# One transition of a fused convolution and expert kernel: the last gate operations wait until block 0 is split

## The chip, the cores and the metric

The kernel runs on one NeuronCore of a Trainium2 chip. The metric is the device time of one execution in microseconds (us); three executions of the kernel before are given, and one more was taken with the hardware profiler. The engines are named as in the profile: PE is TensorE (its weight loads are PEld), DVE is VectorE, ACT is ScalarE, POOL is GpSimd, and SP is SyncE, which issues most of the DMA transfers.

## The reference

A long causal convolution by FFT feeds a two-level mixture of experts. Cut to what matters:

```python
Xf = np.fft.rfft(x, n=2 * S, axis=1)                  # x: (8, 5056, 128)
Hf = np.fft.rfft(h, n=2 * S, axis=0)                  # h: (5056, 128)
x = np.fft.irfft(Xf * Hf[None], n=2 * S, axis=1)[:, :S].reshape(B * S, D)
g_logits = x @ w_group;  g_idx = argmax(g_logits, 1)  # 4 groups, softmax weight g_w
for g in range(4):
    xg = x[g_idx == g]
    e_logits = xg @ w_expert[g]; e_idx = argmax(e_logits, 1)  # 4 experts, weight e_w
    for e in range(4):                                # rows of that expert
        h = np.maximum(xe @ w1[g, e], 0.0)            # 128 -> 1024
        out[tok_idx] = (g_w * e_w)[:, None] * (h @ w2[g, e])  # 1024 -> 128
```

## The kernel before

The eight sequences and the filter h go through in three rounds of three. A round has a first stage (`stage1`, a transform of length 158, 96 steps), then `groups`: for each of 40 pairs of frequencies a forward transform on PE (line 522), two products y and m with the filter's spectrum on DVE (line 540), their sum (line 574), an inverse transform on PE (line 589) and a copy zs on ACT (line 599), which goes to DRAM. The pairs go two by two through a slot of eleven list entries with weights `GW`, 2.0 at the entries 6 and 10 and else 0; so there are 20 slots, p = 0, 2, ..., 38, and a 21st of inverse transforms and stores alone, whose eleven entries (`late(2)`) are run among the first steps of the expert blocks.

A round's second half is its `side`: eight column groups, each with two lumps of inverse transform on PE (lines 723 and 737), transposes and copies of rows (lines 780, 781), the gate's logits (790, 800), and then `gate_math`: some 38 small operations, mostly on DVE (lines 898 to 989), that find each row's expert and its place, with four small count matmuls (lines 975, 976) after eight empty steps. When they are done, the rows are stored by `scatter`, one indirect transfer of POOL for each of 15 columns, with a small cast `pos` before it (line 855, on ACT or DVE); `send` issues the next of them, and `drain` all that are left. A gate operation counts as small: if the list has entries of weight 0 ahead, it is kept in `light` and run one or a few at a time after such entries.

The order of all this is written out: `run` builds one list `main` of (weight, function), and `weave` runs it and lets each side's steps fall due as the weight of the list goes by, from the side's start to its end. The side of round r goes beside round r + 1. The middle side (round two's) starts in round three's first stage and ends at `mark["end", 1]`, which is step 16 - `SIDE1` of the expert blocks.

After round three, `turn` closes the buffers of the rounds and opens those of the experts, `ffn_first(0)` transposes block 0's rows x and splits x and two pieces of its weights in two parts each (a cast on ACT, a subtraction on DVE; lines 1301, 1302), and then the blocks of 512 rows follow with eight steps each: step k does three matmuls of the first layer (`mm1`, lines 1357 to 1359), the split of its result h (lines 1362, 1363), and three of the second layer for two steps before (`mm2`, 1375 to 1377). In steps 0 to 7 of block 0 other splits of weights and of block 1's x fall as well. A block needs a table that tells its expert and its rows; block 0 to 3 have theirs from round one's counts. `table_a`, for the blocks from 4 on, is run seven entries to a step (`NTA`) from the step after the middle side's end: a count `nblocks` with empty entries before its matmul (line 1017), then some 25 small DVE operations, a store of the table to DRAM and a load back (lines 1088, 1093), both on SP. At step 16 SP loads block 4's x (line 1257), which waits for all stores of rounds one and two; `drain` stands at step 15. From step 14 on the last side's lumps run beside the blocks.

Of the kernel before, what the change touches and what calls it, by code (L numbers as in the profile page):

```python
# [46 lines left out]
GW = [0, 0, 0, 0, 0, 0, 2.0, 0, 0, 0, 2.0]  # L47
FW = [0, 0, 1.0, 0, 0, 0, 1.0, 0]
W_S1, W_END = 0.45, 2.5
SIDE0, SIDE1, SIDE2 = 10, 14, 24  # L50
SLOTS = 56
LATE = 4
END0 = 20
# [25 lines left out]
NQ = (NG + 1) // 2  # L79
# [96 lines left out]
def weave(main, sides):  # L176


    light = []

    def flush(n):
        for f in light[:n]:
            f()
        del light[:n]

    room = [0] * (len(main) + 1)
    for i in reversed(range(len(main))):
        room[i] = room[i + 1] + 1 if main[i][0] == 0 else 0
    for i, (w, f) in enumerate(main):
        f()  # L190
        if w == 0:
            flush(-(-len(light) // room[i]))
        for s in sides:
            if s["start"] <= i < s["end"]:
                if i == s["start"]:
                    s["done"] = 0
                    s["acc"] = s["sacc"] = 0.0
                    s["len"] = sum(w for w, _ in main[s["start"]:s["end"]])
                    s["total"] = sum(x[0] for x in s["steps"])
                s["acc"] += w / s["len"]  # L200
                while s["done"] < len(s["steps"]) and (s["sacc"] < s["acc"] * s["total"] - 1e-6 or i == s["end"] - 1):
                    sw, sf, small = s["steps"][s["done"]]
                    if small and room[i + 1] > 0 and i < s["end"] - 1:
                        light.append(sf)
                    else:
                        if small:
                            flush(len(light))
                        sf()
                    s["sacc"] += sw
                    s["done"] += 1  # L210
                if i == s["end"] - 1:
                    flush(len(light))
# [18 lines left out]
class Kernel:  # L231
# [777 lines left out]
    def nblocks(self, x, name):  # L1009
        nc, cp = self.nc, self.tp()  # L1010
        t = cp.tile([128, NE], BF16, name=name + "_m")
        nc.vector.tensor_scalar(t, x, self.iop512, None, op0=ALU.is_gt)
        yield
        for _ in range(8):
            yield
        pr = self.routed()
        nc.tensor.matmul(pr[:, 0:NE], lhsT=self.ones, rhs=t, start=True, stop=True)
        nb = cp.tile([128, NE], F32, name=name)
        nc.vector.tensor_copy(out=nb, in_=pr[:, 0:NE])
        yield  # L1020
        return nb
# [604 lines left out]
    def run(self):  # L1626
        tc = self.tc
        with ExitStack() as ctx:
            self.pools(ctx)
            with ExitStack() as c2:  # L1630
# [7 lines left out]
                side = [self.side(r) for r in range(3)]  # L1638
                main, mark = [], {}

                def add(f, w=0.0):
                    main.append((w, f))

                def late(r):
                    return [f for p in gr[r][1][NQ // 2:] for _, f in p]

                def advance(g):
                    return lambda: next(g, None)
# [11 lines left out]
                for r in range(3):  # L1660
                    if r == 1:
                        add(self.share)
                    pre, steps = gr[r]
                    rest = late(r - 1) if r > 0 else []
                    n = len(s1[r][1])
                    t0 = self.table_0()
                    for k, f in enumerate(s1[r][1]):
                        add(f, W_S1)
                        if r > 0 and k % 2 == 1:
                            add(self.send)  # L1670
                        if r == 0:
                            add(advance(more))
                        if r == 2 and ("end", 0) in mark:
                            add(advance(t0))
                        if k >= 1:
                            for g in rest[RP * k - RP:RP * k]:
                                add(g)
                        if k == SIDE0 and r > 0:
                            add(side[r - 1][0])
                        if k == max(SIDE0 + SIDEG, END0 if r == 2 else 0) and r > 0:  # L1680
                            mark["start", r - 1] = len(main)
                            if r == 2:
                                mark["end", 0] = len(main)
                        if k >= n - PRE and (k - n) % 5 == 0:
                            add(advance(pre))
                    if r > 0:
                        add(lambda: None, W_END)
                    for p in range(0, NQ, 2):
                        for w, f in steps[p // 2]:
                            add(f, w)  # L1690
                        if p >= NQ - LOAD1:
                            add(advance(s1[r + 1][0] if r < 2 else early))
                add(turn)
                add(lambda: self.ffn_first(0))
                rest = late(2)
                ta, tq, tb, fill = self.table_a(), self.table_c(), self.table_b(), self.fill_rows()
                ahead = self.ffn_ahead()
                steps = [f for j in range(NW_MIN) for f in self.ffn_steps(j, (BLK, None) if j else None, NW_MAX)]
                for k, f in enumerate(steps):
# [34 lines left out]
                    if k % 8 == 0 and 0 <= m < TAKE and (m + 1) * n // TAKE > m * n // TAKE:  # L1734
                        add(lambda i=m * n // TAKE: self.take(i))
                weave(main, [
                    dict(start=mark["start", r], end=mark["end", r], steps=side[r][1]) for r in range(3)
                ])
                self.ffn_tail()

# [26 lines left out]
```

## Time and profile before

| | |
|---|---|
| three executions | 1806.07 us median (1799.17, 1806.07, 1806.64) |
| profiled execution | 1805.8 us, its span 1804.1 us |
| PE busy | 1697.4 us, 94% of the span |
| DVE busy | 1298.9 us, 72% |
| ACT busy | 1045.3 us, 58% |
| POOL busy | 759.9 us, 42% |
| mean granted PE clock | 0.979 |

The profiled execution is one of the program on the chip; the span is from its first to its last instruction, and the device time lies 1.7 us above it. Busy is the time in which an engine has at least one instruction at work; the ends of matmuls are modelled, so a busy PE is not a PE at its peak. The granted clock is the share of PE's full 2.4 GHz that the throttle let through.

### The profile page before, as it was taken

What the parts mean: (1) busy time and instruction counts of PE and PEld (TensorE: products, weight loads), DVE (VectorE), ACT (ScalarE), POOL (GpSimd) and SP (SyncE); (2) the same over time, 40 slices, a digit from 0 to 9 for tenths busy, and PEclk for the clock granted to TensorE, in tenths of its full rate; (3) what the DMA queues carried; (4) which work ended last, traced back from release to release, by engine and by line L of the source; (5) the groups of instructions that cost most, each with busy time, mean ns of one, the idle gap of its engine ahead of it and who ended that gap; (6) DMA issues with size and microseconds to landing.
All of it is one profiled execution on the core that took longest, in us unless ns stands there. A gap on an engine that the chain in (4) does not pass through costs nothing. (4 is left out here: it accounts for less than half of the span.)

```text
span 1804.1 us, 49057 instructions
## 1 busy us (share of the span) xinstructions
PE 1697.4 (94%) x17369; PEld 1315.7 (73%) x17369; DVE 1298.9 (72%) x2999; ACT 1045.3 (58%) x2554; POOL 759.9 (42%) x730
## 2 busy tenths in 40 slices
PE   8999888988899888999999999999999999999997
PEld 7667755556665554788777788787788877888987
DVE  6554577774567667677777778777788778787876
ACT  4554443443434344566666667676677767666665
POOL 0451232333144444415454445344555555333444
PEclk9999998998989999999999999999999999999999
DMA  7697676766657766665565554355655575444555
GB/s 211 210 276 210 166 219 202 229 229 191 178 169 234 212 198 224 188 178 171 170 176 169 168 156 144 114 170 182 206 166 155 154 228 181 139 130 144 155 163 157
DMA packets 277994, 330.23 MB, mean 183 GB/s; under 512 B 31863, under 2 KB 210304, under 8 KB 277720
## 3 DMA queue, kind: packets, MB, share of 16 engines
q1 hardware_dynamic: 248856, 270.93, 50.9%
q0 software_dynamic: 20608, 41.79, 6.7%
q10 hardware_dynamic: 8256, 14.10, 2.7%
q8 instruction: 143, 2.34, 0.6%
q14 instruction: 131, 1.07, 0.2%
HBM read 230.35 MB, written 96.86 MB: 181 GB/s over the span
## 5 line engine op out<-in xcount | busy, mean ns | idle before, releaser
L856 POOL DMA_INDIRECT srt<-rw,pos x320 | 339.7, 1062 | 503.8 <-ACT pos L855 130.9
L1428 POOL DMA_INDIRECT out<-orow,at x176 | 182.8, 1038 | 252.9 <-ACT at L1426 199.8
L540 DVE TENSOR_TENSOR y<-pp,hg 128x768 f32<-128x768 f32 (+1 forms) x120 | 103.7, 864 | 123.3 <-PE pp L522 48.0
L1428 POOL DMA_INDIRECT out<-orow,sids x92 | 95.7, 1041 | 123.8 <-DVE orow L1395 79.7
L589 PE MATMUL pp<-y,cg 64*128 64x384 f32 (+1 forms) x752 | 127.9, 466 | 12.9 <-DVE m L540 6.1
L522 PE MATMUL pp<-st,cg 64*64 64x192 f32 (+1 forms) x1588 | 122.4, 416 | 9.1 <-issue 9.0
L599 ACT COPY zs<-pp 128x768 f32<-128x768 f32 (+1 forms) x118 | 85.2, 723 | 72.6 <-PE pp L589 49.5
L439 DVE TENSOR_TENSOR st<-pp,odd 128x320 f32<-128x320 f32 x96 | 46.8, 488 | 101.5 <-ACT odd L438 97.4
L744 ACT COPY yT<-py 128x474 f32<-128x474 f32 (+1 forms) x96 | 44.5, 514 | 124.9 <-PE py L737 108.0
L723 PE MATMUL py<-ig,zm 126*64 126x79 f32 x2048 | 96.7, 241 | 17.2 <-issue 15.5
L1362 ACT ACTIVATE h0h<-px 128x512 fp32r<-128x512 f32 (+1 forms) x109 | 64.0, 587 | 84.3 <-PE px L1359 55.7
L1363 DVE SCALAR_TENSOR_TENSOR h0l<-px,h0h 128x512 fp32r<-128x512 f32 (+1 forms) x109 | 73.3, 673 | 54.5 <-ACT h0h L1362 35.2
L589 PEld LDWEIGHTS pp<-y,cg 64*128 64x128 f32 x752 | 71.9, 190 | 54.0 <-issue 27.6
L723 PEld LDWEIGHTS py<-ig,zm 126*64 126x64 f32 x2048 | 81.6, 141 | 39.4 <-issue 30.9
L540 DVE TENSOR_TENSOR m<-pp,hg 128x768 f32<-128x768 f32 (+1 forms) x120 | 102.7, 856 | 0.2 <-ACT hg L532 0.2
L522 PEld LDWEIGHTS pp<-st,cg 64*64 64x64 f32 x1588 | 60.9, 135 | 55.3 <-issue 42.4
L1363 DVE SCALAR_TENSOR_TENSOR h2l<-px,h2h 128x512 fp32r<-128x512 f32 (+1 forms) x112 | 75.3, 672 | 31.7 <-ACT h2h L1362 18.8
L1363 DVE SCALAR_TENSOR_TENSOR h3l<-px,h3h 128x512 fp32r<-128x512 f32 (+1 forms) x111 | 74.4, 671 | 27.5 <-ACT h3h L1362 26.3
L574 POOL TENSOR_TENSOR y<-y,m 128x512 f32<-128x512 f32 x40 | 50.8, 1275 | 83.0 <-DVE m L562 44.4
L1362 ACT ACTIVATE h3h<-px 128x512 fp32r<-128x512 f32 (+1 forms) x111 | 65.4, 589 | 33.6 <-PE px L1359 24.9
L1363 DVE SCALAR_TENSOR_TENSOR h1l<-px,h1h 128x512 fp32r<-128x512 f32 (+1 forms) x111 | 74.4, 671 | 9.0 <-ACT h1h L1362 3.0
L1362 ACT ACTIVATE h1h<-px 128x512 fp32r<-128x512 f32 (+1 forms) x111 | 65.3, 588 | 20.6 <-PE px L1359 11.5
(477 smaller groups left out, 5200.4 us busy)
## 6 DMA issues: line engine op xcount, KB each, us to landing
wr<-in_moe_w SPq DMA_DIRECT2D x373, 256.0 KB
zd<-zs SPq DMA_DIRECT2D x78, 384.0 KB
zm<-zd SPq DMA_DIRECT2D x64, 378.0 KB
cg<-in_c_g SPq DMA_DIRECT2D x106, 224.0 KB
xr<-srt SPq DMA_DIRECT2D x71, 260.0 KB
hg<-hd SPq DMA_DIRECT2D x80, 128.0 KB
zd<-zs SPq DMA_DIRECT2D x39, 256.0 KB
xt<-in_x ACTq DMA_DIRECT2D x52, 160.0 KB
```

Of the source, the lines that this page charges most:

```text
L439: nc.vector.tensor_tensor(out=all_st[:, 0:2 * HALF, d], in0=even, in1=odd, op=ALU.add)
L522: nc.tensor.matmul(px[c * 64:c * 64 + 64, b, to], lhsT=k, rhs=data[:, of], start=begin, stop=i == len(steps) - 1 or p == 0 and i == 1, til ...
L540: nc.vector.tensor_tensor(out=t[:, :, 0:w].rearrange("p t (r u d) -> p t r u d", r=2, u=nu), in0=taken(px, part).unsqueeze(1).broadcast_to ...
L574: (nc.gpsimd if r == 0 else nc.vector).tensor_tensor(out=y[:, :, 0:w], in0=y[:, :, 0:w], in1=m[:, :, 0:w], op=ALU.add)
L589: nc.tensor.matmul(pz[c][:, 0:w], lhsT=wt[c * 64:c * 64 + 64, k:k + 128], rhs=y[c * 64:c * 64 + 64, part, 0:w], start=part == 0, stop=part ...
L599: nc.scalar.copy(out=z[:, 0:n, 0:w], in_=pp[:, 0:n, 0:w])
L723: nc.tensor.matmul(pys[q][c:c + 64, col(n, u)], lhsT=zms[q][:, n % QB, k:k + 64], rhs=self.ig[:, 0:NH], start=n % QB == 0 and u == 0, stop ...
L744: nc.scalar.copy(out=self.yT[:, k:k + QB * c1], in_=pys.pop(q)[:, 0:QB * c1])
L856: ins = self.nc.gpsimd.indirect_dma_start(out=self.srt, out_offset=bass.IndirectOffsetOnAxis(ap=k["pos"][0:p, j:j + 1], axis=0), in_=k["rw ...
L1362: nc.scalar.activation(out=hh, in_=p, func=AF.Relu)
L1363: nc.vector.scalar_tensor_tensor(out=hl, in0=p, scalar=0.0, in1=hh.bitcast(F32), op0=ALU.max, op1=ALU.subtract)
L1428: ins = self.nc.gpsimd.indirect_dma_start(out=self.a["out"], out_offset=bass.IndirectOffsetOnAxis(ap=ids, axis=0), in_=o, in_offset=None, ...
```

## The change

Two things move. The middle side ends at step 5 of the expert blocks instead of step 2, and `table_a` starts three steps later with it. And from the entry of weight 2.0 at index 6 of round three's second last slot (p = 36) on, the middle side's small steps are kept in `light` without being run, until `ffn_first(0)` has been issued; from there to the side's end one of them is run after each entry of weight 0, and what is left then is run at the end of step 4. Large steps in the hold are run at once. In `table_a` (whose count is named nba) the count's matmul comes sixteen empty entries after its input instead of eight.

```diff
@@ -47,7 +47,7 @@
-SIDE0, SIDE1, SIDE2 = 10, 14, 24
+SIDE0, SIDE1, SIDE2 = 10, 11, 24
@@ -177,6 +177,7 @@
     light = []
+    holds = [s["hold"] for s in sides if "hold" in s]
@@ -188,8 +189,10 @@
     for i, (w, f) in enumerate(main):
         f()
-        if w == 0:
-            flush(-(-len(light) // room[i]))
+        held = any(a <= i < b for a, b in holds)
+        after = any(b <= i < s["end"] for s in sides if "hold" in s for b in (s["hold"][1],))
+        if w == 0 and not held:
+            flush(1 if after else -(-len(light) // room[i]))
@@ -200,10 +203,10 @@
                     sw, sf, small = s["steps"][s["done"]]
-                    if small and room[i + 1] > 0 and i < s["end"] - 1:
+                    if small and (room[i + 1] > 0 or held or after) and i < s["end"] - 1:
                         light.append(sf)
                     else:
-                        if small:
+                        if small and not held:
                             flush(len(light))
                         sf()
@@ -1011,7 +1014,7 @@
-        for _ in range(8):
+        for _ in range(16 if name == "nba" else 8):
             yield
@@ -1686,12 +1689,15 @@
                     for p in range(0, NQ, 2):
-                        for w, f in steps[p // 2]:
+                        for i, (w, f) in enumerate(steps[p // 2]):
+                            if r == 2 and p == NQ - 4 and i == 6:
+                                mark["hold"] = len(main)
                             add(f, w)
                 add(turn)
                 add(lambda: self.ffn_first(0))
+                mark["go"] = len(main)
@@ -1734,7 +1740,10 @@
                 weave(main, [
-                    dict(start=mark["start", r], end=mark["end", r], steps=side[r][1]) for r in range(3)
+                    dict(
+                        start=mark["start", r], end=mark["end", r], steps=side[r][1],
+                        **({"hold": (mark["hold"], mark["go"])} if r == 1 else {}),
+                    ) for r in range(3)
                 ])
```

## Rows read from the trace of the kernel before

**Rows 1.** the page, busy time, share of the span and instructions

```profile
PE 1697.4 (94%) x17369; PEld 1315.7 (73%) x17369; DVE 1298.9 (72%) x2999; ACT 1045.3 (58%) x2554; POOL 759.9 (42%) x730
```

**Rows 2.** timeline of PE: start, length, instruction, [idle before, its releaser]

```profile
708.16 1.20 PE L522 MATMUL pp<-st,cg 64*64 64x384 f32 x16 [1.95 <-issue]
709.16 0.67 PE L522 MATMUL pp<-st,ns 64*64 64x192 f32 x8
...
711.44 0.94 PE L522 MATMUL pp<-st,ns 64*64 64x192 f32 x8
712.31 1.80 PE L589 MATMUL pp<-y,cg 64*128 64x384 f32 x8
715.35 1.56 PE L589 MATMUL pp<-y,cg 64*128 64x384 f32 x8 [1.23 <-DVE m L540]
...
719.38 0.58 PE L1309 MATMUL ptr<-identr,xr 128*128 128x128 f32 x4 [2.14 <-DVE base L980]
```

**Rows 3.** timeline of DVE, last two slots to block 0's split

```profile
705.76 0.96 DVE L540 TENSOR_TENSOR y<-pp,hg 128x768 f32<-128x768 f32 x1 [2.76 <-PE pp L589]
706.64 0.56 DVE L928 TENSOR_REDUCE el<-oh 128x60 f32<-128x240 f32 x1
...
709.84 0.21 DVE L900 TENSOR_TENSOR td<-el,tmx 128x60 f32<-128x60 f32 x1
...
713.31 0.96 DVE L540 TENSOR_TENSOR y<-pp,hg 128x768 f32<-128x768 f32 x1
...
715.12 0.95 DVE L540 TENSOR_TENSOR y<-pp,hg 128x768 f32<-128x768 f32 x1
...
716.85 1.81 DVE L574 TENSOR_TENSOR y<-y,m 128x768 f32<-128x768 f32 x2
718.86 0.17 DVE L979 TENSOR_TENSOR off<-pp,base 128x16 f32<-128x16 f32 x1 [0.19 <-remote]
...
720.86 0.68 DVE L1302 TENSOR_TENSOR x0l<-ptr,x0h 128x512 fp32r<-128x512 f32 x1
```

**Rows 4.** timeline of ACT at the turn

```profile
718.15 0.80 ACT L599 COPY zs<-pp 128x768 f32<-128x768 f32 x1 [1.38 <-issue]
720.04 0.59 ACT L1301 CAST x0h<-ptr 128x512 fp32r<-128x512 f32 x1 [1.09 <-DVE cs L984]
```

**Rows 5.** windows: us, busy PE, PEld, DVE, ACT, POOL (instructions), clock, DMA, GB/s

```profile
720.86:738.81 17.95, 16.92 (x70) 11.37 (x66) 13.59 (x47) 11.88 (x28) 7.44 (x7) 0.94 0.84 238
738.81:748.31 9.50, 9.36 (x75) 7.71 (x77) 9.12 (x21) 6.22 (x16) 5.13 (x6) 1.00 0.39 105
```

**Rows 6.** timeline of DVE, blocks 0 and 1

```profile
728.80 0.17 DVE L1100 TENSOR_TENSOR cnta<-base,base 128x16 f32<-128x16 f32 x1
...
744.00 0.69 DVE L1363 SCALAR_TENSOR_TENSOR h0l<-px,h0h 128x512 fp32r<-128x512 f32 x1
```

**Rows 7.** timeline of PE, blocks 0 to 3

```profile
729.79 0.17 PE L1017 MATMUL py<-nba_m,ones 128*128 128x16 bf16 x1 [0.80 <-DVE cnta L1106]
...
746.27 0.40 PE L1375 MATMUL ptr<-h0h,w3h 128*128 128x512 f32 x1
...
747.06 1.85 PE L723 MATMUL py<-ig,zm 126*64 126x79 f32 x46
...
779.29 0.46 PE L1309 MATMUL ptr<-identr,xr 128*128 128x128 f32 x4
```

**Rows 8.** windows of 1 us, columns as in rows 5

```profile
721.00:722.00 1.00, 1.00 (x6) 0.37 (x4) 1.00 (x2) 0.66 (x2) 0.00 (x0) 0.50 0.77 237
...
729.00:730.00 1.00, 0.21 (x2) 0.21 (x2) 0.93 (x4) 0.00 (x0) 0.73 (x1) 1.00 0.87 235
```

**Rows 9.** waits of SP's queue, 705 to 765 us: total, times, longest

```profile
SPq L1257 <- DMA srt<-rw,pos: 7.6, 1, 7.6
...
SPq L1093 <- DMA tabd<-tab: 3.8, 1, 3.8
```

**Rows 10.** timeline of POOL after step 15

```profile
757.72 1.16 POOL L856 DMA_INDIRECT srt<-rw,pos  x1 [0.31 <-issue]
```

## The prediction

> **What bounds the kernel now.** The page first: TensorE (PE) is busy for 94% of the span [rows 1], so whatever the change frees on VectorE (DVE) is worth only what PE waits for it. The change touches one place, the turn from round three to the expert blocks, so the timelines of PE, DVE and ScalarE (ACT) were read from 700 us on. PE stands idle there three times: 1.95 us before the last slot's first forward transform, 1.23 us for the product m on DVE, and 2.14 us for `base`, which belongs to the last gate operations [rows 2]. DVE has few gaps in the same stretch: the gate operations of the last column group stand between the products and the sums of the last slot, and five lines of them right before x0l, block 0's first split, at 720.86 [rows 3]. So DVE sets much of the turn, and partly with work that block 0 doesn't need.
>
> After that DVE stays nearly full: 13.59 us busy of 17.95 from x0l to step 7's h3l, 9.12 of 9.50 from there to the end of step 14 [rows 5]. The table for later blocks begins there at 728.80 [rows 6]. The strain ends at the lump of the inverse transform on PE at 747.06 [rows 7], for which DVE has nothing to do.
>
> **What is held, and what it costs.** A side's steps follow the weight of the main list. From its start (stage 1's k = 20) to expert step 2 the middle side has 75 x 0.45 + 2.5 + 20 x 4.0 = 116.25 units of weight for its 68.55 of own time; with the end at step 5, which takes in one more unit, 117.25. At the hold 108.25 units are spent, so side time is 63.29 of 68.55. Gate operation k of the last group is due at 62.5 + 0.1366 k: 0 to 5 still run where they do now, 6 to 40 are held. These are 18 steps up to the second reciprocal, eight empty ones, the four count matmuls, five lines more and three empty.
>
> Their DVE time, from start to start: 3.47 us for those from 709.84 to 713.31, 0.56 for `el`, 1.86 for those from 718.86 up to the copies of block 0's ids, which stand right before x0l [rows 3], and three more, put at 0.7 (three times the 0.21 of `td` at least): **6.6 us**. Nothing is removed; these 6.6 us move from before x0l to between x0l and the table.
>
> **What the turn gains.** (a) y of the last slot's first group starts at 713.31, 3.47 us after the gates begin at 709.84 [rows 3], although its forward transform had ended at 709.83 [rows 2]. Without gates the pair of products is limited by the second forward transform, ending at 712.38 [rows 2]; that one starts 0.5 earlier, as `el` no longer stands before the m that frees its bank. So the second y goes from 715.12 to about 711.9, and the sums end at about 715.5 instead of 716.85 + 1.81 = 718.66: 3.2 us. (b) The five lines after the sums, 1.86 us, vanish from before x0l, and the bank that PE waits for 2.14 us is free earlier.
>
> What is late next is ACT: block 0's transposes follow the last inverse transform on PE, and its copy zs starts at 718.15, 1.24 us after its matmuls end by the timeline (715.35 + 1.56), a lag that the profile names issue [rows 2, 4]. If its matmuls follow the inverse before them directly (712.31 + 1.80 - 0.5 = 713.6) with the same lag, the copy starts at about 716.4, the transposes follow it, ACT needs 0.6 for x0h [rows 4], and x0l starts at about 717.6: **3.2 us earlier**. Bounds: 4.8 if the lag goes too (x0l at 716.1), 1.9 if only (b) counts, for instance because the second y waits as its predecessor one slot before did (705.76, 2.76 of idle until an inverse [rows 3]); nothing here excludes that.
>
> **What it gives back.** From x0l on DVE runs in order; I count to the end of step 12's h0l (744.00 + 0.69), the last that PE needs before the lump [rows 6]. Before, that is 23.8 us. After: 13.59 busy in the first stretch [rows 5], less 4.1 of the table, which now starts at step 6, plus its first four operations, 0.8, plus 6.6 of gates: 16.9. Then 8 splits and h operations at 0.61 from start to start, 4.9, and 22 table operations, 3.3 (the table's 31 take 4.9 in all). Sum 25.1, and 0.5 for waits that stay of the 17.95 - 13.59 = 4.4 us of DVE idle: 25.6. PE now starts the matmuls that need this h0l at 746.27, 1.6 us after it is ready, and the lump 0.8 later [rows 7]. That slack is used up: the lump starts 26.4 us after x0l instead of 26.2. So the 6.6 us are paid by 3.9 of DVE idle, by table operations pushed behind the lump and by 1.6 of slack, and the lump gains 3.2 - 0.2, less 0.3 for small ACT waits that I may have missed: **2.7 us** (1.4 to 4.5 by the bounds of x0l). Past the lump PE has gaps of 0.2 to 0.3 us only, so it keeps this.
>
> **Smaller parts.** The eight empty steps more in the table's first count take no time; they move that count's matmul to step 8, behind its input, so PE's wait of 0.80 us for `cnta` [rows 7] goes; that is already in the sum, where DVE is the bound. The count matmuls of the held gates go to the end of step 4 and to another bank; their input is cast three steps ahead, so nothing. The table's round trip through DRAM, on SyncE's queue (SP) with a wait of 3.8 us [rows 9], moves from steps 7 and 8 to 12 and 13, behind block 3's loads and ahead of the second lump's. Table ready at about 717.6 + 25 = 742.5 plus 4.2 is before these loads can go, as they wait for buffers that the first lump frees; some 2 us to spare.
>
> The last group's 15 row stores become due at step 4 instead of the turn: 5 chances fewer, so 9 instead of 4 are left for the drain at step 15. GpSimd (POOL) starts one every 1.3 us, so the last ends about 6.4 later than the 758.88 of now [rows 10], less the gain, and SP's load of block 4, which waits for it (7.6 us now [rows 9]), goes with it, to about 764. PE needs that block at 779.29 [rows 7]; 12 us remain for one transfer: hidden. With 117.25 for 116.25 the middle side also shifts through round three: 12 of its 40 large steps fall later, four by a step of stage 1 and eight by half a slot. No work is added; such a step fills or leaves a PE gap like the 1.95 one, so I allow 2 us either way and forecast nothing.
>
> **The sum.** 1805.8 (profiled execution, its span of 1804.1 and 1.7 around it) - 2.7 = 1803.1; the median shown lies 0.27 above that execution, so 1803.3.
>
> **Rivals.** *The turn is not DVE's.* The lag on zs is PE's own by its name, and the y of the slot before waited until an inverse. If x0l gains only (b), 1.9, and the chain after it costs 0.5 to 1.9 more than before, the result is 1804.4 to 1806: no change.
>
> *All is kept*: x0l at 716.1 and DVE's waits filled, the lump 4.5 earlier: 1801.5. For it: y's 3.47 us are DVE's alone. Against: the lag on zs.
>
> *Slower by the clock.* PE's granted clock was 0.50 (1.2 GHz) at 721 to 722, after the idle of 2.14, and 1.00 through the 0.80 idle at 729 [rows 2, 7, 8]. After the change PE waits for DVE in most steps of block 0; my order of work has one gap of about 1.8 us, before the mm2 of step 3, as step 1's h comes behind 2.1 us of gates. If that takes PE to half clock as the idle of 2.14 does now, a step costs twice its 1.37 us, and a stretch as now from 719.8 to 723 costs 1.6. One such stretch eats over half the gain; two, the second behind the flush at step 4, cost 3.2 and give 1806.5, three 4.8 and 1808.1: some 1807.3. It turns to slower from two stretches on. Against it: the drop of now at 720 to 723 goes where the 2.14 goes.
>
> The Trainium skill, page "TensorE: Matmul & The Clock Gate", section "HAM oscillation — how this bites in real kernels", says that a kernel whose matmuls come in bursts between waits begins each burst at half clock again. By that rule the held gates would cost clock in more than one step of block 0; the trace agrees at the turn (0.50 after 2.14 us of idle), not for the 0.80 us, and no row shows gaps between these.
>
> *It does not do what it says*: only if no gate were due between hold and go; the count above gives 35. Under 0.02, within the first rival.
>
> **How the numbers follow.** Forecast 0.55, the turn not DVE's 0.18, all kept 0.10, clock 0.12, a shift in round three beyond 2 us either way 0.05. The runs shown lie 7 us apart, so the range reaches 3.5 us below "all kept", for a median that falls low, and ends at the clock's time: 1798.0 to 1808.0. A measurement of this kernel tells about 0.5%, 9 us, from no change; no case reaches that but the outer part of the last and a low set of runs: faster 0.06, same 0.89, slower 0.05.
>
> **What the profile after would show.** Right: of the last group only gates 0 to 5 on DVE before block 0's x0l; about 26 us from x0l to the lump; the idle of 1.23 and 2.14 gone; `cnta` behind step 5; nine stores in a row after step 15. Wrong: x0l less than 2 us earlier, counted from the second forward transform; more than 27 us from x0l to the lump; a granted clock of 0.50 between step 0's h0l and the lump; PE waiting for block 4's transposes.

## The result, and the profile after

The changed kernel takes 1817.05 us (median of 14 runs, 1809.55 to 1821.19), the kernel before 1804.01 in the same comparison (14 runs, 1796.23 to 1809.57): ratio 1.0076, 95% interval [1.0059, 1.0092]. It is slower by 13 us, where 2.7 us less were forecast; 1808.0 was the upper end of the range. The profiled execution has a span of 1816.2 us.

The page, busy time of each engine. The instructions are those of before, a few more on DVE and fewer on ACT, and PE's busy time is up by 6.6 us [rows 1]:

```profile
PE 1704.0 (94%) x17369; PEld 1320.2 (73%) x17369; DVE 1299.1 (72%) x3004; ACT 1044.4 (58%) x2549; POOL 758.8 (42%) x730
```

In the changed file each line stands three lines later (L540 is L543, L1302 is L1305, L723 and L737 of the lump are L726 and L740). PE's timeline after, against [rows 2] and [rows 7]:

```profile
712.10 0.98 PE L783 MATMUL py<-ident,yT 128*128 128x128 f32 x7
714.27 1.20 PE L525 MATMUL pp<-st,cg 64*64 64x384 f32 x16 [1.19 <-issue]
...
717.65 1.66 PE L592 MATMUL pp<-y,cg 64*128 64x384 f32 x8 [0.16 <-issue]
720.39 1.56 PE L592 MATMUL pp<-y,cg 64*128 64x384 f32 x8 [1.08 <-DVE m L543]
722.88 0.53 PE L1312 MATMUL ptr<-identr,xr 128*128 128x128 f32 x4 [0.93 <-ACT zs L602]
...
740.18 0.17 PE L1020 MATMUL py<-nba_m,ones 128*128 128x16 bf16 x1 [1.25 <-DVE cnta L1105]
...
751.90 1.31 PE L726 MATMUL py<-ig,zm 126*64 126x79 f32 x32
```

The wait for `base` has gone and a smaller one for zs has come; the wait for m is still there, and so is the wait for the count, larger than before. DVE's timeline after, against [rows 3]:

```profile
712.21 0.96 DVE L543 TENSOR_TENSOR y<-pp,hg 128x768 f32<-128x768 f32 x1 [1.63 <-PE pp L592]
...
718.42 0.96 DVE L543 TENSOR_TENSOR y<-pp,hg 128x768 f32<-128x768 f32 x1 [2.40 <-PE pp L525]
...
720.70 0.96 DVE L543 TENSOR_TENSOR y<-pp,hg 128x768 f32<-128x768 f32 x1 [0.46 <-PE pp L592]
...
724.32 0.68 DVE L1305 TENSOR_TENSOR x0l<-ptr,x0h 128x512 fp32r<-128x512 f32 x1
```

No gate stands between the last slot's products and its sums any more, but DVE now waits for PE. The large loss is further on. POOL's timeline behind step 15, first and last store of the drain, against [rows 10]:

```profile
759.16 0.98 POOL L859 DMA_INDIRECT srt<-rw,pos  x1 [4.00 <-DVE pos L858]
...
769.83 1.01 POOL L859 DMA_INDIRECT srt<-rw,pos  x1 [0.30 <-issue]
```

These are nine stores in a row, as forecast, and SP's load of block 4 waits 14.1 us for them (7.6 before [rows 9]). PE's timeline at the second lump, 96 short matmuls (48 with `zm`, 48 with `zt`):

```profile
762.19 2.29 PE L726 MATMUL py<-ig,zm 126*64 126x79 f32 x48
...
766.34 0.37 PE L740 MATMUL py<-igt,zt 32*64 32x79 f32 x5 [0.36 <-issue]
767.77 0.38 PE L740 MATMUL py<-igt,zt 32*64 32x79 f32 x5 [1.06 <-issue]
769.20 0.54 PE L740 MATMUL py<-igt,zt 32*64 32x79 f32 x4 [1.05 <-issue]
...
772.05 1.07 PE L740 MATMUL py<-igt,zt 32*64 32x79 f32 x21 [0.89 <-issue]
773.06 1.12 PE L1394 MATMUL ptr<-ident,oT 128*128 128x128 f32 x4
...
775.25 0.63 PE L1378 MATMUL pz<-h1h,w2h 128*128 128x512 f32 x1
775.68 0.63 PE L1379 MATMUL pz<-h1h,w2l 128*128 128x512 f32 x1
```

While POOL issues its stores, PE gets through one to five matmuls of the lump's second half and then stands, naming no releaser ("issue"). The lump lasts from 762.19 to 773.12, 10.93 us; before, the same lump, at 756.66, took 3.85. The last store ends at 770.84, and from 772.05 on 21 matmuls follow in 1.07 us. The ordinary matmuls behind it start 0.43 us apart. Windows from x0l on with the lengths of those in [rows 5], then the second lump, its two parts before and after the clock falls, and what follows it (columns as in [rows 5]):

```profile
724.32:742.27 17.95, 15.70 (x70) 10.48 (x67) 16.74 (x50) 10.53 (x24) 1.00 (x1) 1.00 0.92 275
742.27:751.77 9.50, 8.67 (x43) 6.72 (x41) 8.95 (x36) 6.25 (x17) 4.89 (x5) 1.00 0.58 165
762.19:773.12 10.93, 6.25 (x98) 4.64 (x98) 1.29 (x2) 0.70 (x3) 6.82 (x7) 0.79 0.15 48
762.19:768.40 6.21, 3.83 (x67) 2.96 (x66) 1.29 (x2) 0.54 (x2) 4.83 (x5) 1.00 0.16 54
768.50:773.10 4.60, 2.40 (x31) 1.66 (x31) 0.00 (x0) 0.14 (x1) 1.99 (x2) 0.50 0.13 41
773.10:778.60 5.50, 5.50 (x17) 4.50 (x16) 1.38 (x2) 2.10 (x6) 1.00 (x1) 0.50 0.79 233
```

The granted clock is 1.00 from x0l to the first lump; in the second lump it is 1.00 up to 768.40 and 0.50 from 768.50 on, and it stays at 0.50 for 5.5 us behind it. Seven stores overlap the lump for 6.82 us, and the DMA engines are busy for only 0.15 of it: the data of the stores is not what fills the time.

A ledger by the start of the same instructions in each trace: the last product of the third last slot (the 235th of y and m on DVE, counting the three small ones of p = 0) to block 0's x0l, in the table "products to x0l"; x0l to the first lump; first lump to second; second lump to the third x0l; from there to the end.

| profile | products to x0l | x0l to lump 1 | lump 1 to 2 | lump 2 to third x0l | sum | to the end |
|---|---|---|---|---|---|---|
| before | 23.84 | 26.20 | 9.60 | 23.75 | 83.39 | 1023.7 |
| after | 23.20 | 27.58 | 10.29 | 33.45 | 94.52 | 1020.6 |

Of the 12.1 us between the spans, 11.1 lie here, and 9.7 of them behind the start of the second lump: 7.1 in it, about 2.5 by the half clock (twelve matmuls 0.43 instead of 0.23 apart, four transposes 0.4 longer). The 4.1 us lost before the stretch (it begins at 701.1 instead of 697.0) are not explained; the place scatters, since in the fifth comparison below it begins at 700.6 and 697.6 in two kernels that are alike up to there. The 3.1 regained after it have no explanation here: this one profile of before has 1023.7, three of changed kernels on such chips have 1018.2 to 1020.6.

### The profile page after: what moved, and what is told of

Its sections match the earlier page's. It is cut to its first block, busy times and chain, and to the rows that moved or that the text cites. A ratio compares the mean times of both kernels' runs of the same rounds, so it can differ in the third digit from the quotient of the medians.

```text
span 1816.2 us, 49062 instructions
## 1 busy us (share of the span) xinstructions
PE 1704.0 (94%) x17369; PEld 1320.2 (73%) x17369; DVE 1299.1 (72%) x3004; ACT 1044.4 (58%) x2549; POOL 758.8 (42%) x730
## 3 DMA queue, kind: packets, MB, share of 16 engines
q14 instruction: 131, 1.07, 0.2%
## 5 line engine op out<-in xcount | busy, mean ns | idle before, releaser
L543 DVE TENSOR_TENSOR y<-pp,hg 128x768 f32<-128x768 f32 (+1 forms) x120 | 103.8, 865 | 134.8 <-PE pp L525 49.9
L726 PE MATMUL py<-ig,zm 126*64 126x79 f32 x2048 | 97.3, 242 | 18.7 <-issue 18.0
L726 PEld LDWEIGHTS py<-ig,zm 126*64 126x64 f32 x2048 | 82.6, 142 | 40.7 <-issue 35.1
L543 DVE TENSOR_TENSOR m<-pp,hg 128x768 f32<-128x768 f32 (+1 forms) x120 | 103.0, 858 | 0.0
```

The costliest lines, as they stand in the source:

```text
L543: nc.vector.tensor_tensor(out=t[:, :, 0:w].rearrange("p t (r u d) -> p t r u d", r=2, u=nu), in0=taken(px, part).unsqueeze(1).broadcast_to ...
L726: nc.tensor.matmul(pys[q][c:c + 64, col(n, u)], lhsT=zms[q][:, n % QB, k:k + 64], rhs=self.ig[:, 0:NH], start=n % QB == 0 and u == 0, stop ...
```

## The experiments

The texts on record before the runs compare three theories. **Theory A**: the stores in POOL's queue hold PE's lump; the change piles nine of them on the second one. **Theory B**: the held gates and the turn cost the time by themselves. **Theory C**: a longer drain costs in any case, because block 4 arrives later. The texts do not keep to these letters: C is the shift through round three in the first comparison and a lump held alike on every chip in the second, and B in the third says that the sign of the change does not hang on the chip.

Five comparisons were made, each on one chip with the kernel before beside it. In the first four the kernel before took 1691.41, 1692.89, 1691.46 and 1691.14 us, in the fifth 1806.12. They are called the 1692 and the 1806 comparisons. The result above belongs to the second kind. The first and the fifth bear the same chip number, so the number alone does not tell the two apart.

**First comparison (1692).** Four kernels. The changed one with a store at every step from 5 to 14 (A's remedy):

```
-                    elif k < 8 * (NA - 2) and k % 8 not in (3, 4, 5, 6):
+                    elif k < 8 * (NA - 2) and (5 <= k < 15 or k % 8 not in (3, 4, 5, 6)):
```

> The changed kernel, with one row store sent after each of the steps 5 to 14, so that some 3 and not 9 are left for the drain at step 15; held gates, side's end and table stay as changed. Theory A (the nine stores of the drain lie on the second lump of the inverse transform and stop PE there, 7 us and 2.5 more at half clock after it): second lump back from 10.9 us to 3.5 to 4.5, ratio to the kernel before 1.001 to 1.003 instead of 1.0076. Theory B (the held gates load DVE in block 0): second lump is a by-product, ratio stays at 1.006 to 1.008. Theory C (the later end of the side shifts round three): ratio stays at 1.006 to 1.008.

The kernel before with no store sent from the turn to step 5, so that its drain has nine:

```
     def send(self, eng="v"):
-        if self.sends:
+        if self.sends and not self.hush:
...
                 def turn():
+                    hush(True)
...
+                    if k == 5:
+                        add(lambda: hush(False))
```

> The kernel before, with the five row stores between the turn and step 5 withheld, so that the drain at step 15 has 9 instead of 4; nothing else changes. Theory A: the second lump goes from 3.9 to 8 to 11 us, ratio 1.004 to 1.006. Theories B and C: gates, side and table are as before, ratio 0.999 to 1.001.

The changed kernel with the last side's lumps eight steps later (`START2 = 22` for 14):

> The changed kernel, with the last side's lumps started eight steps later (START2 22 for 14), so that the drain of nine runs beside expert steps alone. Theory A: the stores cost PE little there (a step stays at 1.4 to 1.5 us), lumps stay at 2.9 to 3.9, ratio 1.001 to 1.003. If a store costs PE its time beside any work, steps 15 to 23 take some 8 us longer and the ratio stays at 1.006 to 1.008. Theories B and C: 1.006 to 1.008.

The kernel before with the middle side's end alone moved (`SIDE1` 11 for 14):

> The kernel before, with only the middle side's end moved from step 2 to 5 (SIDE1 11 for 14): no hold, eight empty steps in the table's count. The last group's stores become due after step 2, so the drain has about 9 here too. Theory A: second lump 8 to 11 us, ratio 1.004 to 1.006. Theory B (the hold): 0.999 to 1.001. Theory C (the shift through round three): 1.006 to 1.008 with a second lump below 5.

Measured, as ratios to the kernel before: spread 0.9974 [0.9955, 0.9992], nine in the drain 1.0005 [0.9989, 1.0021], late lump 1.0073 [1.0056, 1.0089], side's end alone 0.9989 [0.9976, 1.0003]. The nine stores of the second kernel meet a lump of 3.60 us, which has a wait for its own load inside, and cost nothing that can be told, so A's price (1.004 to 1.006) was not there on this chip. The side's end alone has nine stores in its drain too and a lump of 3.45 us, where A had 8 to 11. The late lump lost for a reason of its own, which PE's timeline of that kernel shows:

```profile
678.87 1.85 PE L726 MATMUL py<-ig,zm 126*64 126x79 f32 x24 [6.04 <-DMA zm<-zd]
```

PE stands 6.04 us for the lump's own load and the granted clock is 0.50 through the lump: that kernel tells nothing on the stores. What the unchanged change does on such a chip was the open question.

**Second comparison (1692).** The changed kernel as it is, the spread and the nine once more, and the hold alone (the changed kernel with `SIDE1` back at 14):

> The changed kernel itself, as it is. The theories price what the chip makes of a PE lump (96 matmuls, 2.84 us alone) under POOL's row stores. A (the loss is the second lump under the drain's nine stores, and a chip sets how much a store holds PE): where the kernel before takes about 1804 us, ratio 1.0076 with a second lump near 11 us; where it takes about 1691 us, the second lump takes 3 to 5 us and the ratio is 0.998 to 1.002. B (the held gates themselves and the turn cost the time, whatever the chip): ratio 1.006 to 1.009 on either. C (the second lump is held alike on every chip): second lump 9 to 12 us and ratio 1.004 to 1.008 on either.

> The changed kernel with a store sent at every step from 5 to 14 of block 0, so that the drain behind step 15 has two or three stores instead of nine. A: where the kernel before takes about 1804 us, second lump about 3 us, ratio 0.999 to 1.003, that is 0.005 to 0.008 below the changed kernel as it is; where it takes 1691 us, 0.996 to 0.999, at most 0.003 below it. B: as the changed kernel as it is, within 0.002. C: 0.004 to 0.007 below it on either chip.

> The changed kernel with block 1's table started where it started before (SIDE1 14 for 11): the hold alone. The rows are taken three steps earlier, so the later sends find more slots and the drain holds about eight stores. A: the second lump is held nearly as in the changed kernel (8 to 11 us at 1804 us), ratio 1.005 to 1.008 there, 0.998 to 1.002 at 1691 us. B: 1.006 to 1.009. If the table's later start is what costs: 1.000 to 1.003 on either.

> The kernel before with no store sent from the turn to step 5, so that its drain holds nine stores, without the hold. A: second lump 7 to 11 us and ratio 1.003 to 1.006 where the kernel before takes about 1804 us; 0.999 to 1.002 where it takes 1691 us. B: 0.999 to 1.001 on either. C: 1.003 to 1.006 on either.

Changed kernel 0.9956 [0.9936, 0.9976], spread 0.9964 [0.994, 0.9988], hold alone 0.9986 [0.9965, 1.0007], nine 0.9997 [0.9974, 1.002]. The same change that lost 0.76% gains 0.44% here. B and C fall for this group. A had 0.998 to 1.002 for the changed kernel here, so the gain itself was not expected by any of the three. The hold alone and the side's end alone show no gain that is clear of noise.

**Third comparison (1692).** The changed kernel and the spread again, one profile of the kernel before, and the kernel before with the spread's line alone:

> The changed kernel as it is, once more, since the first two chips gave the kernel before 1691 and 1693 us and the result was taken at 1804 us. A (a chip sets how much a store of POOL holds a PE lump): with the kernel before near 1804 us, ratio 1.006 to 1.009 and a second lump of 8 to 12 us; near 1692 us, ratio 0.994 to 0.998 and a second lump of 2.84 us. B (the sign of the change does not hang on the chip; the two comparisons differ by chance of the layout of that run): 0.994 to 0.998 on either.

> The kernel before as it is, for its profile on the chip of the three others. A: near 1692 us its lumps take 2.84 us with up to three stores beside them, and the turn (x0l to lump 1) is as in the first profile, about 26 us; near 1804 us the lumps show the first profile's lengths. Ratio 1.000 by either theory.

> The changed kernel with a store at every step from 5 to 14 of block 0 (drain of two or three). A: near 1804 us 0.005 to 0.008 below the changed kernel as it is, second lump about 3 us; near 1692 us within 0.002 of it. B: within 0.002 of it on either.

> The kernel before with the same denser sends from step 5 to 14 and no hold: its four last stores leave the drain. A: near 1804 us the second lump falls from 3.85 to 2.84 us and one or two lumps of the last slots are untouched, ratio 0.998 to 1.000; near 1692 us 0.999 to 1.001, so that the hold alone keeps its 0.003 to 0.004 in the spread kernel. B: 0.999 to 1.001 on either.

Changed kernel 0.9954 [0.9937, 0.9971], spread 0.996 [0.9946, 0.9974], spread without hold 1.0 [0.9985, 1.0015]. So the gain comes with the change and not with where the stores go. The profile of the kernel before shows that its second lump waits here too, but for its load (PE's timeline):

```profile
661.77 1.04 PE L723 MATMUL py<-ig,zm 126*64 126x79 f32 x24 [1.93 <-DMA zm<-zd]
663.62 1.04 PE L723 MATMUL py<-ig,zm 126*64 126x79 f32 x24 [0.80 <-DMA zm<-zd]
```

**Fourth comparison (1692).** The changed kernel again; with no store between the turn and the drain; with the hold from the last slot only; and with the count's empty steps back at 8:

```
     def send(self, eng="v"):
-        if self.sends:
+        if self.sends and not self.hush:
...
     def drain(self):
+        self.hush = False
...
                 def turn():
+                    self.hush = True
```

```
-                            if r == 2 and p == NQ - 4 and i == 6:
+                            if r == 2 and p == NQ - 2 and i == 0:
```

```
-        for _ in range(16 if name == "nba" else 8):
+        for _ in range(8):
```

> The changed kernel as it is, beside the three below on one chip. A (the sign hangs on whether a POOL store holds a PE lump on that chip): near 1692 us for the kernel before 0.994 to 0.998; near 1804 us 1.006 to 1.009.

> The changed kernel with no store sent between the turn and the drain behind step 15, so that the drain holds some fifteen stores instead of nine (the suspected cost made larger). A: near 1692 us, where a lump with three stores beside it takes its 2.84 us, the stores cost PE nothing and the ratio stays within 0.002 of the changed kernel as it is; near 1804 us the second lump stays held for all the stores beside it (11 to 18 us) and the ratio is 1.007 to 1.013. C (a longer drain costs by itself, since the rows of block 4 arrive later): 0.003 or more above the changed kernel on any chip.

> The changed kernel with the hold begun at the last slot of round three instead of the second last: half of the hold. Where the changed kernel gains 4.5 us between the second last slot and x0l (3.5 in the slots' products, 1.0 between the last product and x0l), this one keeps the 1.0 and loses the part of the 3.5 that belongs to the second last slot, about half: ratio 0.001 above the changed kernel's, 0.995 to 0.999. If the two slots' gain comes from elsewhere: as the changed kernel, or as the kernel before.

> The changed kernel with the block count's 16 empty steps put back to 8, so that the count's matmul comes eight small operations sooner. If PE's wait for the count (1.25 us at step 6 in the changed kernel's profile) is what the later place costs or saves: the wait moves or grows to about 2 us and x0l to the first lump changes by less than 1.5 us; ratio within 0.001 of the changed kernel.

Changed kernel 0.9965 [0.9949, 0.9981], all in the drain 0.999 [0.9971, 1.0008], last slot 0.9961 [0.9946, 0.9975], count early 0.9962 [0.9944, 0.9979]. Here is the second lump of the changed kernel under the same nine stores. PE's timeline:

```profile
657.25 1.86 PE L726 MATMUL py<-ig,zm 126*64 126x79 f32 x48
659.04 1.05 PE L740 MATMUL py<-igt,zt 32*64 32x79 f32 x48
```

POOL's timeline, the fourth store of the nine and the last:

```profile
658.32 1.13 POOL L859 DMA_INDIRECT srt<-rw,pos  x1 [0.30 <-DVE h2l L1366]
...
664.89 1.01 POOL L859 DMA_INDIRECT srt<-rw,pos  x1 [0.30 <-DVE w0l L1305]
```

And the window of the lump (columns as in [rows 5]):

```profile
657.25:660.09 2.84, 2.84 (x98) 2.66 (x98) 1.29 (x2) 0.53 (x2) 2.23 (x3) 1.00 0.17 57
```

The same 98 instructions, the same stores, POOL busy for 0.79 of the lump, the DMA share nearly that of the result's profile (0.17 and 0.15), and PE has no gap: 2.84 us for 10.93. With fifteen stores in the drain the lump still takes 2.84 us, so A held for the lump; yet this kernel lies 0.0025 above the changed one, between A's 0.002 and C's 0.003, with intervals that overlap. Its ledger loses 2.7 us between the second lump and the third x0l, and the trace shows C's way to it: SP's load of block 4 waits 22.4 us for the stores instead of 14.2, SP issues the next loads of expert weights behind that wait, from 674.40 on, and ACT waits for one of them (ACT's timeline):

```profile
678.51 0.62 ACT L1306 CAST w0h<-wr 128x512 fp32r<-128x512 f32 x1 [3.02 <-DMA wr<-in_moe_w]
```

The changed kernel has no such wait there. PE loses its time behind the third x0l, 1.15 us of it for h3l at 685.24.

The ledger of the 1692 profiles:

| profile | products to x0l | x0l to lump 1 | lump 1 to 2 | lump 2 to third x0l | sum | to the end |
|---|---|---|---|---|---|---|
| before | 20.94 | 25.28 | 10.44 | 23.76 | 80.42 | 1001.1 |
| before, `SIDE1` 11 | 20.76 | 25.55 | 8.43 | 23.35 | 78.09 | 1001.5 |
| changed, fourth | 16.46 | 27.61 | 8.44 | 22.74 | 75.25 | 1000.6 |
| hold alone | 16.58 | 26.36 | 8.43 | 23.63 | 75.00 | 1002.3 |
| last slot | 18.80 | 24.73 | 8.43 | 22.74 | 74.70 | 1000.7 |
| count early | 16.46 | 29.24 | 8.44 | 22.74 | 76.88 | 1002.5 |
| all in drain | 16.46 | 27.18 | 8.43 | 25.40 | 77.47 | 1002.3 |

Products to x0l gain 4.5 us, of which 2.3 are given back before the first lump. Holding only the last slot's gates gains 2.1 and gives nothing back, so both arrive at the second lump within 0.6 us of each other: by these two profiles the second last slot's hold is worth nothing, where I had expected 0.001, which the ratios can't tell. The later count is worth 1.6 us of this stretch (27.61 against 29.24), a little more than the 1.5 that I had as the limit. PE waits 2.49 us for it when it comes early and 1.24 when late, and behind the longer wait the granted clock is 0.50. The window in count early:

```profile
641.70:645.00 3.30, 3.30 (x9) 2.55 (x9) 2.40 (x10) 0.68 (x2) 1.00 (x1) 0.50 0.77 190
```

The changed kernel's clock stays at 1.00 there. The ratio can't tell the 1.6 us.

**Fifth comparison (1806).** The changed kernel and the spread once more:

> The changed kernel as it is, a fifth time, for the chip that it falls on. A: kernel before near 1692 us, 0.994 to 0.998; kernel before near 1804 us, 1.006 to 1.009 and a second lump of 8 to 12 us.

> The changed kernel with a store at every step from 5 to 14 of block 0, beside it on the same chip. A: near 1692 us within 0.002 of the changed kernel; near 1804 us 0.005 to 0.008 below it, with a second lump of about 3 us.

Changed kernel 1816.22 us, 1.0064 [1.0037, 1.009]; spread 1814.88, 1.0051 [1.002, 1.0082]. The sign is that of the result again. The changed kernel's second lump, PE's timeline:

```profile
765.97 0.39 PE L740 MATMUL py<-igt,zt 32*64 32x79 f32 x5 [0.38 <-issue]
767.40 0.38 PE L740 MATMUL py<-igt,zt 32*64 32x79 f32 x5 [1.04 <-issue]
768.83 0.54 PE L740 MATMUL py<-igt,zt 32*64 32x79 f32 x4 [1.05 <-issue]
...
771.68 1.09 PE L740 MATMUL py<-igt,zt 32*64 32x79 f32 x23 [0.89 <-issue]
```

It takes 11.01 us, and from its middle on the pattern is that of the result's profile to a few hundredths. The spread kernel did not do what A expected of it (0.005 to 0.008 below): it gained 0.0013. Its second lump is free, 2.84 us, but the stores now meet the first one. PE's timeline there, and the windows of that lump and of what follows:

```profile
748.26 1.86 PE L726 MATMUL py<-ig,zm 126*64 126x79 f32 x44
...
751.97 0.36 PE L740 MATMUL py<-igt,zt 32*64 32x79 f32 x5 [0.37 <-issue]
752.69 0.39 PE L740 MATMUL py<-igt,zt 32*64 32x79 f32 x5 [0.36 <-issue]
753.43 0.37 PE L740 MATMUL py<-igt,zt 32*64 32x79 f32 x4 [0.36 <-issue]
```

```profile
748.26:757.40 9.14, 5.77 (x98) 4.09 (x97) 2.43 (x6) 0.65 (x4) 5.61 (x6) 0.88 0.40 110
757.40:761.50 4.10, 4.10 (x10) 3.24 (x11) 0.87 (x4) 1.68 (x4) 1.83 (x2) 0.50 0.35 110
```

| profile | products to x0l | x0l to lump 1 | lump 1 to 2 | lump 2 to third x0l | sum | to the end |
|---|---|---|---|---|---|---|
| changed, fifth | 23.31 | 27.56 | 10.29 | 31.99 | 93.15 | 1018.2 |
| spread, fifth | 23.28 | 27.38 | 16.91 | 22.74 | 90.31 | 1019.1 |

Behind the second lump 9.3 us are saved, but 6.6 of them are lost behind the first; 2.8 remain in the sum, about what the ratios show. Both lumps together, beyond twice 2.84 us, against the stores' overlap with them: before 2.2 for 3.9, after 9.9 for 9.5, changed in the fifth 10.0 for 9.5, spread 6.3 for 5.6. That is A's mechanism in four profiles of the 1806 kind, and moving the stores moved the hold from one lump to the other; what failed is the remedy. In the 1692 kind the changed kernel's two lumps have 4.5 us of stores beside them and lose nothing.

## Why the prediction was wrong, point by point

**The failed step** is in "Smaller parts": nine stores in the drain, "12 us remain for one transfer: hidden". The count, nine, was right. But I looked only at who waits for the stores' data, block 4's load, and not at what PE does while they are issued. What stood in the place of zero: 7.1 us of lump and some 2.5 us at half clock behind it in the result's profile, 7.2 and some 1.1 in the fifth comparison. In the kernel before, the store of [rows 10] stands inside the second lump, and that lump already has gaps without a releaser. Its rows on PE:

```profile
756.66 1.85 PE L723 MATMUL py<-ig,zm 126*64 126x79 f32 x46
758.70 0.30 PE L723 MATMUL py<-ig,zm 126*64 126x79 f32 x2 [0.19 <-issue]
...
759.45 1.05 PE L737 MATMUL py<-igt,zt 32*64 32x79 f32 x45 [0.18 <-issue]
```

It took 3.85 us where the third one, at 787.44 without a store beside it, takes 2.84; I had not set the two rows side by side.

**The turn** was mis-sized, and the place before it was left out. I put x0l 3.2 us earlier. In the 1692 comparisons products to x0l are 4.5 us shorter, near the upper bound of 4.8; in the result's profile 0.6. The 0.6 has two parts. From the first product of the second last slot to x0l the stretch shrinks by 4.3 us, as it does in the 1692 comparisons (16.99 us before, 12.63 in the fourth). The windows of that stretch, before and after:

```profile
700.75:720.86 20.11, 14.71 (x119) 8.91 (x113) 16.63 (x41) 6.88 (x23) 9.62 (x10) 0.84 0.61 203
708.50:724.32 15.82, 11.04 (x94) 6.28 (x92) 11.32 (x19) 6.33 (x19) 9.17 (x10) 1.00 0.50 156
```

DVE is rid of 5.3 us of work there, and the granted clock is 1.00 instead of 0.84; how much of the 4.3 us is the clock's is not shown. My own working of x0l was short at one step: from the copy zs to x0l I had 1.2 us, and it takes 2.3 (722.03 to 724.32), because block 0's transposes wait for that copy. The other part, 3.7 us, is lost before a gate is held: the first product of that slot comes 7.39 us after the last one of the slot before, 3.74 in the kernel before. A sign of being wrong that I had named shows in the result's profile: counted from the last slot's second forward transform, x0l is less than 2 us earlier (6.83 us after its end instead of 8.48). The rival "the turn is not DVE's" is right in what DVE waits for, PE's transforms, 4.27 us in front of 708.50 and 2.40 in front of 718.42. In the second last slot those transforms run while POOL issues eight stores in a row. PE's timeline in the fifth comparison's changed kernel:

```profile
704.20 1.40 PE L525 MATMUL pp<-st,cg 64*64 64x384 f32 x15
705.80 0.32 PE L525 MATMUL pp<-st,cg 64*64 64x192 f32 x1 [0.21 <-issue]
705.83 0.52 PE L525 MATMUL pp<-st,ns 64*64 64x192 f32 x3
706.53 0.55 PE L525 MATMUL pp<-st,ns 64*64 64x192 f32 x4 [0.17 <-issue]
707.25 0.32 PE L525 MATMUL pp<-st,ns 64*64 64x192 f32 x1 [0.17 <-issue]
```

The product before it and the next one stand 7.45 us apart there, 3.83 in the changed kernel of the fourth comparison, where stores lie over these transforms too. It looks like the pattern in the lump, on longer matmuls. That the stores are the cause here too is read from where they lie; no run took them away. PE's delay is not all of it either: its second transform takes 3.37 us from 704.20 on instead of 1.47, 1.9 more, and the product comes 3.6 later. The rest is not settled.

**What it gives back**: 26.4 us from x0l to the lump forecast, 27.6 measured in both kinds, so 1.2 too little, and more than the 27 that I had named as a sign of being wrong. I had PE's wait for `cnta` vanish; it is 1.25 us, because DVE begins the count only at 739.04, with gates and block 0's operations before it. PE also waits 0.78 us for h1l and 0.83 for h3l in that stretch; the kernel before has 0.80 for `cnta` and 0.36 for h3l. **The clock rival** did not come where I put it: the clock is 1.00 from x0l to the first lump. It came in the held lump, from 768.50 on, and lasted 5.5 us beyond it. A wait in block 0 did cost clock in count early, 2.49 us for the count, but no wait in the changed kernel's block 0 was that long. The Trainium skill, page "TensorE: Matmul & The Clock Gate", section "HAM oscillation — how this bites in real kernels", says that a kernel whose bursts of matmuls are parted by long enough waits begins each burst at half clock. The trace agrees in part: the bursts of the lump from 768.50 on ran at 0.50, those before, behind gaps of up to 1.06 us, at 1.00.

**Round three's shift** of up to 2 us was the right size in the 1692 kind: the side's end alone gives 0.9989, 1.9 us, with an interval that holds zero. In the 1806 kind it was not run alone; whether the 3.7 us in front of the hold belong to it is open.

**The sum**, by the ledger: forecast -2.7; result's profile -0.6 at the turn (-4.3 and +3.7), +1.4 to the first lump, +0.7 in it, +9.7 from the second on, together +11.1. In the 1692 comparisons -4.5, +2.3, -2.0, -1.0, together -5.2 against the one profile of the kernel before (-2.8 against the one with `SIDE1` 11), where the ratios say -5.9 to -7.8.

**What stays open**: why PE is held under stores in one kind of comparison and not in the other. The two kinds differ in the whole kernel (1692 and 1806 us), and so do PE's waits for "issue": the changed kernel has 16.7 us in 37 of them at L726 and 12.2 in 29 at L740 in the fifth comparison, none and 2.1 in 2 in the fourth. Nothing that was varied here sets it. A version that keeps the hold and sends the nine stores in steps that touch neither lump was not run, so whether the change can win in both kinds is open too. In the 1692 kind no version that was run beats the changed kernel by more than the noise.

## What to carry to other kernels

A transfer is not hidden because its data is wanted late: set the rows of the issuing engine beside those of the engine that bounds the kernel, and look whether short instructions there run slower under it, as the lump of 3.85 us instead of 2.84 already told in the kernel before. When work is put off, list everything that comes due with it and where the heap lands; spreading it can move the heap to the next sensitive place. A change of half a per cent is worth comparing on several occasions before it is kept or dropped.

## What the hardware showed that was not expected

- The same kernel takes 1691 to 1693 us in four comparisons and 1804 to 1806 in two, with the same instructions; the same change has ratio 0.9954 to 0.9965 in three of the first kind and 1.0064 and 1.0076 in the second.
- In the second kind, 96 short matmuls (2.84 us alone) take 10.9 us under back-to-back indirect stores of POOL: one to five matmuls, then a gap, each packet some 0.72 or 1.43 us after the last, while the stores start every 1.28 us and the DMA engines are 0.15 busy. The Trainium skill, page "Perfetto Trace Analysis", section "DMA Instruction — SWDGE (GPSIMD)", says that the span shown for such an instruction ends when its descriptors are written, not when the data has moved. No row read here tells when these stores' data moved, and what in them holds PE no run here shows.
